# Moving the planned place of a few TensorE steps in an attention and mixture-of-experts kernel

## The chip, the cores and the metric

The kernel runs on one core of one Trainium2 chip. The metric is device time of one execution in microseconds; a run's time is a median over executions. The kernel before has a median of 804.08 us in 3 runs (800.58 to 804.29).

## The reference, cut to what matters

```python
def reference(q, k, v, w_gate, w1, w2):      # q, k, v: [8, 8, 576, 64]
    scores = q @ k.T / 8, masked in blocks of 64
    x = softmax(scores) @ v                  # as rows: [4608, 512]
    logits = x @ w_gate                      # 8 experts
    # pairs (row, expert) by falling logit; a row goes to the first expert
    # that still has room; each expert takes cap = 4608 // 8 = 576 rows
    for e in range(8):
        h = np.maximum(x[assigned == e] @ w1[e], 0.0)    # 512 -> 1024
        out[assigned == e] = h @ w2[e]                   # 1024 -> 512
```

The assignment is exact: an expert fills up, its rows leave the competition, and the next expert to fill is found.

## The kernel before, in words

**Two stages.** Attention comes first (to about 340 us in the profile) and writes its rows x in a high and a low float16 half to DRAM. Then come eight rounds k = 0 to 7, each with a routing and the products of one expert. A round's number is the order in which experts fill up, so expert 0 in this text is the first one to fill.

**Routing (`route`, `invert`).** For k < 7 a search of 14 steps finds the expert that fills next and its threshold. Each step is two counts on VectorE (L776, L777), one on ScalarE (L750) and a small matmul that adds them up (`tot`, L791), so it goes round three engines. Then VectorE makes a mask, a group of matmuls gives each chosen row its place in the list (`po`, L852 to L859), VectorE turns the places into one-hot tables (L870, L872, L893 `OH`, L897 `OL`, L899 and L900 `RH`), 36 matmuls invert them (`pe`, L908), 8 more finish the list of rows (`ps`, L915), and VectorE writes it as `ix` (L918). The last routing (k = 7) has no search, since one expert is left, but all that comes after.

**Gathering (`gather`, `flip`).** Five indirect DMAs on GpSimd (L980) fetch the 576 rows of an expert as `xg`: four of 128 rows and one of 64. For k = 0 and 1 TensorE transposes each (`xt`, 8 matmuls, L990), and ScalarE (L994) and VectorE (L995) each copy one half of the result into `X`. For k > 1 a DMA on SyncE transposes (L1005).

**Weights (`weights`).** Eight loads of 512 KB (L966, SyncE) into six buffers `raw`; for the first four loads of rounds 0 and 1 ScalarE and VectorE convert (L938, L940), else ScalarE (L945, L949) and GpSimd (L951).

**Products (`ffn`).** First `h` (L1030): 8 groups over the first 256 columns of X, which needs only the first two gathered blocks, then 8 over the other 320 (128 and 448 in round 0). ScalarE and VectorE write each group out as `HH` and `HL` (L1016, L1018). Then `y`: four blocks of 128 rows, each 8 steps of 3 matmuls (L1055), and the block m = 4 with the last 64 rows, 4 steps of 6 matmuls at half width (L1059). A result leaves through ScalarE (L1038, for m = 4 also VectorE, L1042) and an indirect DMA on GpSimd (L1046). PSUM has four buffers `g` for h and y.

**What sets the order.** Every engine carries out its instructions in the order in which the program holds them, and that order is made at build time by a planner (`Sched`). Each strand of the work is a generator that names an engine, a cost in ns and the events that it waits for; `Sched.run` takes the strand that could start first by its own clock, and lets one of higher priority (smaller number) go first where it becomes ready soon enough: for TensorE in this stage, more than 500 ns (`ST`) before the other would have ended. A strand that has been ready for over 300 ns (`WAIT`) is not held back further. Transposes have priority 1, products 3, routing 0. The planner's clock is a guess: on the chip, semaphores hold the instructions until their inputs are there, in the planned order.

A gather tells the planner by `soft` (L65) when its rows will have landed: `q`, the planner's clock of the DMA queue, is set to the later of `q` and now plus `lat` (1100 ns), plus a cost of 728 ns, and the event stands 950 ns after that. `hold` (L886) sets an event that the matmuls `po` (L848) and `pe` (L903) of a routing wait for; it is called once ahead of each of the two.

Of the kernel before, what the change touches and what calls it, by code (L numbers as in the profile page):

```python
# [614 lines left out]
class Moe:  # L615
# [269 lines left out]
        yield from s.invert(k,L16,h2)  # L885
    def hold(s,k):  # L886

        s.sc.ev['hold',k]=s.sc.now+(8000 if k==s.E-1 else 0)
    def invert(s,k,L16,h2):
        nc=s.nc; rp=s.rp; C=s.C; V=nc.vector; sc=s.sc  # L890
        yield D,440
# [80 lines left out]
    def gather(s,k,ix):  # L972
        nc=s.nc; fp=s.fp; sc=s.sc
        tl=[]
        for m in range(5):
            n=P if m<4 else 64
            yield G,1038,('ffn',k-2),('xm',k-1,m)
            if m==0: X=s.X[k]=fp.tile([P,8,576],F16,tag="X",name=f"X{k}")
            xg=fp.tile([P,1024],F16,tag="xg",name=f"xg{k}_{m}",bufs=5)
            nc.gpsimd.indirect_dma_start(out=xg[:n],out_offset=None,in_=s.xd,in_offset=bass.IndirectOffsetOnAxis(ap=ix[:n,m:m+1],axis=0))  # L980
            sc.soft(728,('xg',k,m))
            sc.nolat()
            if m==4: sc.set(('gi',k))
            sc.add(s.flip(k,m,n,xg,X),1,sc.now)
# [138 lines left out]
```

## Time and profile before

| what | value |
| --- | --- |
| median of 3 runs | 804.08 us (800.58 to 804.29) |
| the profiled execution's own time | 801.86 us |
| its span, first to last instruction | 800.1 us |
| TensorE busy, share of the span | 717.8 us, 90% |
| VectorE, ScalarE, GpSimd busy | 585.0, 545.1, 467.0 us |
| mean granted TensorE clock | 0.965 |

The span is what the trace covers; 1.76 us of the profiled execution lie outside it. The median of the runs is 2.2 us above the profiled execution, which lies inside their spread. PE stands for TensorE, DVE for VectorE, ACT for ScalarE, POOL for GpSimd, SP for SyncE; a row of a timeline has the start in us, the duration in us, engine, line, operation, output and inputs, a shape, a count, and in brackets the idle time of the engine ahead of it and what ended that. In a timeline, neighbouring instructions of the same line and tiles are merged.

### The profile page before, as it was taken

How to read it: one execution, taken by the hardware profiler on the slowest of the kernel's cores; microseconds unless marked ns; L12 is line 12 of the kernel's file. 1: busy time of each engine (PE TensorE's matmuls, PEld its weight loads, DVE VectorE, ACT ScalarE, POOL GpSimd, SP SyncE). 2: the span in 40 equal slices, each digit the busy share in tenths (PEclk: the TensorE clock that was granted, in tenths of full speed). 3: DMA queues.
4: the chain of work that ended last, by engine and by line, in shares of the span. 5: the costliest groups of instructions: out<-in, count | busy, mean ns of one | idle time of the engine just before them, and what ended most of it. 6: DMA issues, size and time to landing. Idle time of an engine off the chain costs nothing.

```text
span 800.1 us, 19136 instructions
## 1 busy us (share of the span) xinstructions
PE 717.8 (90%) x6539; PEld 479.6 (60%) x6539; DVE 585.0 (73%) x2395; ACT 545.1 (68%) x1476; POOL 467.0 (58%) x509
## 2 busy tenths in 40 slices
PE   5889998899999999913898999999999999999995
PEld 3666676677767767601644755747557475574752
DVE  6899798988889799488787977969777683730210
ACT  5789888888988888533745859496775947392210
POOL 5788888897889876212324337475471926873001
PEclk9899999999999999955899999999999999999998
DMA  9879999999999991324408049291845819861001
GB/s 203 157 145 179 213 203 209 164 176 204 230 164 222 188 198 35 99 80 133 138 14 294 25 139 231 74 295 42 254 129 184 179 49 273 270 162 40 20 15 45
DMA packets 244305, 121.51 MB, mean 152 GB/s; under 512 B 200816, under 2 KB 227312, under 8 KB 244208
## 3 DMA queue, kind: packets, MB, share of 16 engines
q1 hardware_dynamic: 238320, 101.42, 56.1%
q0 software_dynamic: 5888, 18.88, 7.4%
q8 instruction: 51, 0.84, 0.4%
q14 instruction: 46, 0.38, 0.2%
HBM read 71.32 MB, written 18.87 MB: 113 GB/s over the span
## 4 chain that ended last, share of the span: by engine, by line
PE 58%; DVE 19%; DMA 8%; ACT 8%; issue 3%; POOL 3%; SPq 1%; POOLq 0%; DVEq 0%; ACTq 0%
PE h L1030 23%; PE y L1055 16%; PE psb L463 5%; DVE m L405 5%; PE psb L380 4%; DMA kT<-k 4%; PE psb L498 4%; ACT P L416 4%; DVE kS L350 2%; POOL P L438 2%; PE y L1059 2%; DMA xg<-x,ix 2%; ACT PT L444 2%; DVE jk L776 1%; DMA raw<-in_moe_w_dram 1%
## 5 line engine op out<-in xcount | busy, mean ns | idle before, releaser
L438 POOL TENSOR_TENSOR P<-P,m 128x320 f32<-128x320 f32 (+8 forms) x285 | 209.3, 769 | 48.2 <-DVE m L430 28.4
L1030 PE MATMUL h<-X,W 128*128 128x320 f16 (+3 forms) x1536 | 195.1, 287 | 0.0
L1030 PEld LDWEIGHTS <-W 128*128 128x128 f16 x1536 | 142.2, 98 | 42.7 <-issue 3.1
L416 ACT ACTIVATE P<-psb,m 128x576 f32<-128x576 f32 (+8 forms) x288 | 149.2, 542 | 25.8 <-DVE m L409 19.7
L1055 PE MATMUL y<-W,HH 128*128 128x512 f16 x512 | 152.2, 379 | 0.0
L951 POOL TENSOR_TENSOR W<-raw,W 128x1024 f16<-128x1024 f32 x56 | 118.4, 2136 | 40.6 <-ACT W L949 38.3
L405 DVE TENSOR_REDUCE m<-psb 128x1 f32<-128x576 f32 (+8 forms) x288 | 125.0, 481 | 12.4 <-PE psb L380 11.9
L463 PE MATMUL psb<-mident,P 128*128 128x128 f32 x800 | 106.0, 281 | 10.9 <-POOL P L438 3.6
L1046 POOL DMA_INDIRECT out_dram<-yo,ix x40 | 39.4, 986 | 113.1 <-ACT yo L1038 79.2
L380 PEld LDWEIGHTS <-qT 128*64 128x64 f16 x1408 | 78.1, 112 | 42.8 <-issue 27.8
L380 PE MATMUL psb<-kT,qT 128*64 128x288 f16 (+8 forms) x704 | 91.7, 286 | 10.2 <-ACT P L416 9.7
L463 PEld LDWEIGHTS psb<-mident,P 128*128 128x128 f32 x800 | 87.3, 142 | 22.5 <-POOL P L438 6.4
L498 PE MATMUL psb<-PT,V 128*64 128x448 f32 (+5 forms) x776 | 97.2, 388 | 2.4 <-DVE PT L446 1.9
L980 POOL DMA_INDIRECT xg<-x,ix x40 | 41.6, 1040 | 95.8 <-DVE ix L918 37.7
L1055 PE MATMUL y<-W,HL 128*128 128x512 f16 x256 | 97.0, 379 | 0.0
L1016 ACT ACTIVATE HH<-h 128x320 f16<-128x320 f32 (+3 forms) x128 | 52.1, 410 | 63.9 <-PE h L1030 59.5
L444 ACT ACTIVATE PT<-psb 128x512 f32<-128x512 f32 (+1 forms) x165 | 82.4, 592 | 5.8 <-PE psb L463 5.6
L380 PE MATMUL psb<-kS,qT 128*64 128x288 f16 (+8 forms) x704 | 84.4, 284 | 1.6 <-DVE kS L350 1.5
L1018 DVE SCALAR_TENSOR_TENSOR HL<-h,HH 128x320 f16<-128x320 f32 (+3 forms) x128 | 56.9, 452 | 38.5 <-ACT HH L1016 38.2
L1055 PEld LDWEIGHTS <-HH 128*128 128x128 f16 x512 | 46.9, 98 | 52.6 <-issue 2.0
L945 ACT ACTIVATE raw<-raw 128x512 f32<-128x512 f32 x112 | 67.4, 626 | 6.6 <-DMA raw<-in_moe_w_dram 6.5
L498 PEld LDWEIGHTS psb<-PT,V 128*64 128x64 f32 x776 | 49.5, 137 | 33.5 <-issue 24.3
(204 smaller groups left out, 1074.9 us busy)
## 6 DMA issues: line engine op xcount, KB each, us to landing
raw<-in_moe_w_dram SPq DMA_DIRECT2D x64, 512.0 KB, 5.5
x<-XR SPq DMA_DIRECT2D x8, 1152.0 KB, 5.7
kn<-in_k_dram SPq DMA_DIRECT2D x15, 576.0 KB, 5.1
qn<-in_q_dram SPq DMA_DIRECT2D x15, 576.0 KB, 7.1
V<-in_v_dram SPq DMA_DIRECT2D x64, 128.0 KB, 4.4
V<-in_v_dram SPq DMA_DIRECT2D x16, 64.0 KB, 3.9
xg<-x,ix POOLq DMA_INDIRECT x40, 4.3
out_dram<-yo,ix POOLq DMA_INDIRECT x40, 2.8
```

The costliest lines, as they stand in the source:

```text
L380: nc.tensor.matmul(out if len(K1.shape) == 2 else out.rearrange("p (r j) -> p r j", r=2), lhsT=A[:, h, 64 * i:64 * i + 64], rhs=K1, start= ...
L405: nc.vector.tensor_reduce(m[:, 0, c:c + 1], ps[:, o:o + 64 * (i + 1)] if g else s.part(ps, g, i, o), axis=AX.X if g else AX.XY, op=OP.max)
L416: nc.scalar.activation(out, in_, AF.Exp, bias=m[:, 1, c:c + 1], scale=s.ESC, accum_out=m[:, 2, c:c + 1])
L438: nc.gpsimd.tensor_tensor(sl, sl, m[:, 3, c:c + 1].to_broadcast([P, w]), op=OP.mult)
L444: s.nc.scalar.activation(out, in_, AF.Copy)
L463: nc.tensor.transpose(ps[:, a], s.Pb[n % s.NP][:, s.OFF[i] + 128 * j:s.OFF[i] + 128 * j + P], s.ident)
L498: nc.tensor.matmul(ps[64 * h:64 * h + 64, 64 * (i0 - b0):64 * (b1 - b0)], lhsT=vn[:, j, 2 * (n % 2) + h, :], rhs=pt[:, s.PTI[(j, i0)]:s.PT ...
L945: nc.scalar.activation(raw[:,x],raw[:,x],AF.Copy,scale=s.WS)
L951: nc.gpsimd.tensor_tensor(lw,raw,hi,op=OP.subtract)
L1018: nc.vector.scalar_tensor_tensor(HL[:,f,ts],ps,0.0,HH[:,f,ts],op0=OP.max,op1=OP.subtract)
L1030: nc.tensor.matmul(ps,lhsT=W[:,a,d,f*P:f*P+P],rhs=X[:,4*(d//2)+d%2+l,ts],start=(d==0 and n==0),stop=(d==3 and n==2))
L1055: if m<4: nc.tensor.matmul(ps,lhsT=Z[:,f,m*P:m*P+P],rhs=Y[:,a,f],start=(f==n==0),stop=(f==7 and n==2))
```

## The change

Two numbers that only the planner reads are changed. No instruction is added, removed or altered; only the order of the instructions on the engines can differ.

```diff
     def hold(s,k):
 
-        s.sc.ev['hold',k]=s.sc.now+(8000 if k==s.E-1 else 0)
+        s.sc.ev['hold',k]=s.sc.now+(10000 if k==s.E-1 else 0)
...
             nc.gpsimd.indirect_dma_start(out=xg[:n],out_offset=None,in_=s.xd,in_offset=bass.IndirectOffsetOnAxis(ap=ix[:n,m:m+1],axis=0))
-            sc.soft(728,('xg',k,m))
+
+            sc.soft(728,('xg',k,m),4600 if k==1 else 1100)
             sc.nolat()
```

The first edit is about the last routing (k = 7): each of `po` and `pe` is held for 10.0 us of the planner's clock instead of 8.0. The second is about the second expert (k = 1): its gathers count as landed at the earliest 4600 + 728 + 950 ns after their issue instead of 1100 + 728 + 950 ns. By its description the change puts the products of the first expert's last 64 rows ahead of the transposes of the second expert's rows, and the last routing's matmuls later.

## The prediction

> **What bounds the kernel now.** I read the page first, then busy time by stage, then TensorE's waits, and last the timelines of the two places that the change touches.
>
> ```profile
> PE 717.8 (90%) x6539; PEld 479.6 (60%) x6539; DVE 585.0 (73%) x2395; ACT 545.1 (68%) x1476; POOL 467.0 (58%) x509
> core 0: us, PE busy (x) PEld busy (x) DVE busy (x) ACT busy (x) POOL busy (x), PEclk, DMA share, GB/s
> 432.90:443.63 10.73, 6.92 (x72) 3.65 (x71) 7.85 (x37) 5.20 (x13) 4.17 (x4) 1.00 0.64 231
> 443.63:493.33 49.70, 49.70 (x384) 30.64 (x382) 41.12 (x225) 38.99 (x96) 24.38 (x16) 1.00 0.46 140
> engine line waited for: us in total, times, longest us
> PE xt L990 <- DMA xg<-x,ix: 3.5, 3, 1.7
> PE pe L908 <- DVE RH L900: 1.3, 1, 1.3
> PE tot L791 <- ACT ja L750: 1.3, 2, 0.7
> ```
>
> In the expert stage TensorE is the bound: from 443.63 to 493.33 it is busy for all 49.70 us. So time is won only where it stands still, and a microsecond won there reaches the end unless something else becomes late. The waits (window 432.9 to 700) name the places. Two belong to the change: 3.5 us in front of `xt`, the transposes of the second expert's rows, all in the stretch 432.90 to 443.63 (6.92 busy of 10.73), and 1.3 us in front of `pe` of the last routing. The third, 1.3 us, is the search, in the rounds between. Nothing else is above 0.2. So the stretch from 443.63 to the last routing is almost solid, and what the change can win lies in 3.5 + 1.3 us and what hangs on them. The clock is 1.00 in both stretches shown, so a shorter wait changes no clock.
>
> **Edit for k = 1: products ahead of transposes.** TensorE's order at that place:
>
> ```profile
> 434.86 0.62 PE L990 MATMUL xt<-m_idh,xg 128*128 128x128 f16 x8 [1.75 <-DMA xg<-x,ix]
> 436.29 0.62 PE L990 MATMUL xt<-m_idh,xg 128*128 128x128 f16 x8 [0.81 <-DMA xg<-x,ix]
> 436.75 0.59 PE L1055 MATMUL y<-W,HH 128*128 128x512 f16 x2
> 438.53 0.62 PE L990 MATMUL xt<-m_idh,xg 128*128 128x128 f16 x8 [0.97 <-DMA xg<-x,ix]
> 440.12 1.03 PE L990 MATMUL xt<-m_idh,xg 128*128 128x128 f16 x16
> 441.09 0.62 PE L1059 MATMUL y<-W,HH 128*64 128x512 f16 x4
> 441.76 0.60 PE L1059 MATMUL y<-W,HH 128*64 128x512 f16 x4
> 443.63 1.81 PE L1030 MATMUL h<-X,W 128*128 128x256 f16 x15
> 432.95 0.95 POOL L980 DMA_INDIRECT xg<-x,ix  x1 [0.30 <-issue]
> 434.20 1.23 POOL L980 DMA_INDIRECT xg<-x,ix  x1 [0.30 <-issue]
> DMA to landing us min/median/max: 7.1/7.1/7.1
> DMA to landing us min/median/max: 6.5/6.5/6.5
> ```
>
> (The last four rows are the gathers of the fourth and fifth block, and what the view of line 980 gives for each alone.) In the old order the last product step of block m = 3 and the four steps of the last 64 rows (L1059) stand between and behind the transposes, while TensorE stands at transposes whose rows haven't landed. The planner had expected them 1100 + 728 + 950 = 2778 ns after the issue; with the change it expects them at 6278 ns at the earliest, close to the 6.5 and 7.1 us above. The shift is at most 3.5 us. The five product steps need 5 x 0.67 = 3.3 us (the step at 441.76 follows the one at 441.09 by 0.67; the step of m = 3 is taken alike). So all of them just fit ahead.
>
> What then bounds the start of `h` at 443.63? The transposes still can't run before their rows land, and the landing doesn't move: the gathers are issued on POOL by 435.4, before anything differs. From 434.86 - 1.75 = 433.11, where the old order fell idle, TensorE has 3.3 us of products and two transposes at 1.03 / 2 = 0.52, together 4.4 us: done by 437.5, the first landings (434.86, 436.29) long past, with 1.0 us to spare for two small `tot`. The third transpose waits for its landing at 438.53, the fourth for 432.95 + 7.1 = 440.05, the fifth for 434.20 + 6.5 = 440.7. It ends at 440.7 + 0.5 = 441.2, and `h` follows: 443.63 - 441.2 = **2.4 us earlier**. The bounds: if the planner keeps one product step of 0.67 behind the last transpose, 1.7; if it also lets steps of `h`, whose first half needs two blocks only, into the waits for the fourth and fifth, all the idle time of the stretch, 10.73 - 6.92 = 3.8, can go. I take 2.4, the row of the last landing, since the shift of 3.5 barely exceeds the 3.3 us of work: little is left to slip in front.
>
> `h` needs two more things. Its weights:
>
> ```profile
> 440.23 1.22 DVE L940 SCALAR_TENSOR_TENSOR W<-raw,W 128x1024 f16<-128x1024 f32 x1
> 463.41 2.13 POOL L951 TENSOR_TENSOR W<-raw,W 128x1024 f16<-128x1024 f32 x1 [1.16 <-ACT W L949]
> 471.89 0.59 PE L1055 MATMUL y<-W,HH 128*128 128x512 f16 x2
> ```
>
> The last conversion of W1 ends at 441.45 on DVE, queued behind the copies out of `xt`; with the copies planned later it can only move forward, and where it stays it costs 0.2. The last conversion of W2 ends on POOL at 465.54, and its first user, the seventh step of `y`, stands at 471.89: 6.35 us of cover. PE comes 2.4 us earlier, and the planner, which has the loads behind the transposes, may order the conversions up to 3.5 us later: 0.4 are left, so I cost it at nothing. The copies (L994, L995) stand later on ACT and DVE; the search step behind them, whose `tot` stands behind the first transpose in PE's queue until now, comes earlier, so nobody waits for the move. The `g` buffers that m = 4 and `h` take over were emptied before, except block m = 3's, which now ends earlier. The queues passed are PE, ACT and DVE; SP and POOL hold nothing that the move passes.
>
> **Edit for the last routing.** VectorE and GpSimd there, with the same two instructions one round earlier in the first two rows:
>
> ```profile
> 659.56 0.18 DVE L870 TENSOR_SCALAR h<-q 128x36 f16<-128x36 f32 x1
> 661.55 0.75 DVE L897 TENSOR_TENSOR OL<-m_iom,L 128x1152 f16<-128x1152 f16 x1
> 680.04 0.18 PE L853 MATMUL po<-MM,m_tri 128*128 128x36 f16 x1
> 680.55 5.25 DVE L870 TENSOR_SCALAR h<-q 128x36 f16<-128x36 f32 x1
> 686.41 5.38 DVE L897 TENSOR_TENSOR OL<-m_iom,L 128x1152 f16<-128x1152 f16 x1
> 692.16 0.40 DVE L900 TENSOR_SCALAR RH<-OH,m_pc 128x720 f16<-128x720 f16 x1
> 679.46 6.30 POOL L951 TENSOR_TENSOR W<-raw,W 128x1024 f16<-128x1024 f32 x3
> 686.96 4.21 POOL L951 TENSOR_TENSOR W<-raw,W 128x1024 f16<-128x1024 f32 x2
> 692.61 0.91 PE L908 MATMUL pe<-RH,OL 128*32 128x40 f16 x36 [1.35 <-DVE RH L900]
> 693.45 0.62 PE L1059 MATMUL y<-W,HH 128*64 128x512 f16 x4
> 696.44 23.69 PE L1030 MATMUL h<-X,W 128*128 128x256 f16 x192
> 710.68 6.31 SPq L1005 DMA_TRANSPOSE X<-xg  x4
> 743.50 23.69 PE L1030 MATMUL h<-X,W 128*128 128x256 f16 x192
> ```
>
> Between `po` and `RH` lie 12.5 us, of which two instructions take 10.6 instead of 0.9: each ends when a run of POOL's L951 ends (685.80 beside 679.46 + 6.30 = 685.76; 691.79 shortly behind 686.96 + 4.21 = 691.17). The planner knows nothing of this; it puts `pe` 8 us behind its own end of `RH`, and PE stands for 1.35 us. With the change `po` moves 2.0 us back (to 682.0) and `pe` 4.0, since its hold counts from steps that follow `po`: from its old place, 691.26, to about 695.2, behind the four steps of the last 64 rows and one or two of expert 6's `h`.
>
> When is `RH` ready then? L870 comes to 682.6, still within POOL's run until 685.76; so all behind it stays, and `RH` ends at 692.56: cover 2.7 us. If instead these instructions take 10.6 us of themselves, `RH` ends 2 us later, at 694.6, and 0.6 us of cover are left. Either way the wait of **1.35 us goes**; for it to stay whole, `RH` would have to come 4 us late, so the term lies between 0 and 1.35. The Trainium skill ("SBUF — State Buffer", section "Terms") has VectorE and GpSimd share a port pair that is locked for a whole instruction, while the loser blocks; by it the first reading holds, by the plain durations the second, and with 0.6 us to spare instead of 2.7 this term would be less sure. The ends at 685.80 and 685.76 agree with the rule.
>
> What `pe` passes, and what its followers pass, costs nothing: the list `ix` feeds the gathers of expert 7, whose `h` starts at 743.50; the last of its transposing DMAs is issued by 710.68 + 6.31 = 717.0, which leaves 26 us, and 4 are used. POOL's stores and conversions queued behind the gathers serve the same `h` or the output of rows long done.
>
> **Sum.** 801.86 - 2.4 - 1.35 = 798.1 for an execution like the profiled one; that one lies 2.2 us under the median of the runs, so the median becomes 804.08 - 3.75, rounded **800.4 us**, 0.47% less. About 0.5%, 4.0 us, is what a measurement of this kernel can tell from no change.
>
> **Rivals.** *More idle time goes*: `h` fills the waits between landings (3.8 instead of 2.4), and the search, no longer held up behind transposes, takes away its 1.3 later on: 804.08 - 3.8 - 1.35 - 1.3 = 797.6. For it: routing runs on with less delay. Against: the plan's shift hardly exceeds the work.
>
> *The change does only half*: the transposes stay in front, or the 2.4 us are taken back by the W2 conversions, whose cover falls to 0.4. Then 804.08 - 1.35 = 802.7. The planner's 500 ns rule, which lets a transpose past a step that it would meet, speaks for the first; the 0.4 still being cover, against the second.
>
> *A descriptor delay*: the gather at 430.69 took 1.95 us on POOL where that at 432.95 took 0.95. If rearranged DVE work does this to the last one, `h` loses 1.0: 801.4. L940 moves forward, and its like ran there (430.60 in the row below). The Trainium skill ("SBUF — State Buffer", section "SBUF: two separate sides") lets some VectorE instructions keep GpSimd from writing the descriptors of its DMAs; these two rows agree. Against: by the old trace DVE comes to its next L940 only after the last gather's issue.
>
> ```profile
> 430.60 1.22 DVE L940 SCALAR_TENSOR_TENSOR W<-raw,W 128x1024 f16<-128x1024 f32 x1
> 430.69 1.95 POOL L980 DMA_INDIRECT xg<-x,ix  x1 [0.30 <-issue]
> 587.65 0.16 PE L791 MATMUL tot<-cn,m_bo 128*128 128x3 f16 x1 [0.58 <-ACT ja L750]
> 579.14 6.20 DMA raw<-in_moe_w_dram
> ```
>
> *Slower*: the planner's moved clock gives experts 2 to 6 another order. SP issues loads and transposing DMAs in one queue; at 579.14 a load came late behind them and took 6.20 us; ACT had to wait for it, a sign count stood behind that on ACT, and PE stood for the count (0.58 at 587.65). If one more DMA that waits for a gather comes ahead of such a load, ACT stands up to 6.2 us and PE 5.6 more than now. It decides from 3.75 us on: once is 804.08 - 3.75 + 5.6 = 805.9, twice 811.5. Against it: a planned tie that has to fall badly, and `mid` ties each routing to the products two rounds before, so that shifts don't add up.
>
> **Chances.** Forecast 0.50, more goes 0.22, half or a delay 0.18, slower 0.10 (0.07 of it past 0.5%). The forecast's 0.47% lies just under the bound, so about four in ten of it count as faster; with nearly all of the second case: faster 0.42, same 0.51, slower 0.07. Range: down to 797.6 and a little for the spread of 0.2% in the runs, 796.8; up to no gain, 804.1.
>
> **What would show it.** Right: no wait of `xt` above 1.1 us and together under 2; five product steps ahead of the second transpose; `h` of expert 1 at about 441.2; no wait at `pe`, with L1059 all in front of it; L870 still ending with POOL's run; `h` of expert 6 at 692.7, the span 796.4. Wrong: `h` of expert 1 at 443 or later, new waits on `raw` or on W2 in PE's list between 443 and 690, or `RH` behind `pe` again.

## The result, and the profile after

| | before | changed |
| --- | --- | --- |
| median | 804.18 us (6 runs, 800.58 to 807.52) | 811.95 us (6 runs, 810.18 to 814.58) |
| ratio to before | | 1.0109, 95% interval 1.0083 to 1.0135 |
| span of the profiled execution | 800.1 us | 810.4 us |
| mean granted TensorE clock | 0.965 | 0.957 |

The changed kernel is 1.1% slower; 0.47% faster was forecast. Lines from L981 on stand one later in the changed kernel (`h` is L1031, the 64-row steps L1060, stores L1047). First its list of TensorE's waits, for the window 420 to 812: engine, line, what it waited for, us in total, times, longest.

```profile
PE h L1031 <- POOL W L951: 7.4, 1, 7.4
PE tot L791 <- ACT ja L750: 4.8, 6, 1.7
PE xt L991 <- DMA xg<-x,ix: 1.7, 3, 1.1
PE tot L791 <- DVE jk L777: 0.3, 1, 0.3
```

Against the list of before, the wait of `pe` (1.3) is gone and that of `xt` halved (3.5 to 1.7): both intended effects are there. New is one wait of 7.4 us of `h` for a weight conversion on GpSimd, and the search's waits, `tot`, grew from 1.5 (1.3 + 0.2) to 5.1. Next TensorE's timeline of the changed kernel, at the place of the edit for k = 1 and at the long wait.

```profile
434.33 0.62 PE L1060 MATMUL y<-W,HH 128*64 128x512 f16 x4
435.75 0.62 PE L991 MATMUL xt<-m_idh,xg 128*128 128x128 f16 x8
436.30 0.62 PE L1060 MATMUL y<-W,HH 128*64 128x512 f16 x4
...
440.85 0.62 PE L991 MATMUL xt<-m_idh,xg 128*128 128x128 f16 x8 [1.06 <-DMA xg<-x,ix]
441.33 0.81 PE L1031 MATMUL h<-X,W 128*128 128x256 f16 x6
...
493.03 0.16 PE L791 MATMUL tot<-cn,m_bo 128*128 128x3 f16 x1 [1.10 <-ACT ja L750]
493.06 1.36 PE L1031 MATMUL h<-X,W 128*128 128x256 f16 x11
501.81 1.04 PE L1031 MATMUL h<-X,W 128*128 128x256 f16 x4 [7.39 <-POOL W L951]
707.00 0.92 PE L908 MATMUL pe<-RH,OL 128*32 128x40 f16 x36
```

`h` of the second expert starts at 441.33 (before 443.63). `h` of the third starts at 493.06, still 0.27 us ahead of before, does 11 matmuls, and stands until 501.81. Why, GpSimd's timeline tells, first of the changed kernel, then of before:

```profile
484.73 6.31 POOL L951 TENSOR_TENSOR W<-raw,W 128x1024 f16<-128x1024 f32 x3
491.20 1.00 POOL L1047 DMA_INDIRECT out_dram<-yo,ix  x1 [0.17 <-issue]
498.64 0.96 POOL L1047 DMA_INDIRECT out_dram<-yo,ix  x1 [6.43 <-DMA X<-xg]
499.62 6.29 POOL L951 TENSOR_TENSOR W<-raw,W 128x1024 f16<-128x1024 f32 x3
```

```profile
484.19 2.15 POOL L951 TENSOR_TENSOR W<-raw,W 128x1024 f16<-128x1024 f32 x1
486.51 1.01 POOL L1046 DMA_INDIRECT out_dram<-yo,ix  x1 [0.17 <-ACT W L949]
487.55 6.32 POOL L951 TENSOR_TENSOR W<-raw,W 128x1024 f16<-128x1024 f32 x3
494.03 1.01 POOL L1046 DMA_INDIRECT out_dram<-yo,ix  x1 [0.17 <-issue]
499.55 0.96 POOL L1046 DMA_INDIRECT out_dram<-yo,ix  x1 [4.52 <-ACT HH L1016]
```

W1 of an expert is four conversions (L951), and the fourth is wanted by the 12th matmul of `h`. Before, all four ended by 493.87, ahead of the stores of the second expert's third and fourth block. Now three stand ahead of the two stores and the fourth behind them, at 499.62. The second store waits 6.43 us, and the conversion, ready long since, waits in GpSimd's queue behind it. The chain of waits of the changed kernel (start, duration, what) runs through the first store's landing:

```profile
491.20 6.67 DMA out_dram<-yo,ix
...
498.64 0.96 POOL out_dram L1047
...
499.62 2.14 POOL W L951
...
501.81 1.04 PE h L1031 x4
```

The clock adds to it. Windows of the changed kernel, with the columns of the prediction's second view:

```profile
494.00:496.00 2.00, 0.42 (x4) 0.12 (x2) 1.76 (x9) 2.00 (x6) 0.00 (x0) 0.80 1.04 265
496.00:498.00 2.00, 0.00 (x0) 0.00 (x0) 0.00 (x0) 0.13 (x1) 0.00 (x0) 0.50 1.00 134
501.80:506.00 4.20, 4.19 (x24) 3.10 (x25) 1.95 (x11) 2.87 (x7) 4.11 (x2) 0.57 0.02 6
```

TensorE works from 501.80 to 506.00 at 0.57, so 4.20 x 0.43 = 1.8 us of work are lost there. The DMA share of about 1.0 while the store is under way says that the 16 DMA engines were busy throughout, with the transposing DMAs among the rest; that this made the landing late (6.67 us, where the profile's page gives 2.7 as the median of all 40 stores) is argued, not shown. The Trainium skill ("DMA: Bandwidth & Descriptors", section "Anatomy of one DMA — SWDGE (gpsimd) path") says that a DMA's semaphore wait happens on the sequencer that issues it, ahead of its dispatch; the 6.43 us on POOL, with work behind them, agree.

**The balance.** Stall 7.4, lost clock 1.8, search 5.1 - 1.5 = 3.6, less 1.8 at the transposes and 1.3 at `pe`: 9.7 of the 810.4 - 800.1 = 10.3 us between the spans. The two spans are single executions, and the medians lie 7.8 us apart, so this is an account of the profiles and not of the medians.

### The profile page after: what moved, and what is told of

Read it like the earlier page. It is cut to its first block, busy times and chain, and to the rows that moved or that the text cites. A ratio compares the mean times of both kernels' runs of the same rounds, so it can differ in the third digit from the quotient of the medians.

```text
span 810.4 us, 19131 instructions
## 1 busy us (share of the span) xinstructions
PE 718.8 (89%) x6539; PEld 480.0 (59%) x6539; DVE 579.1 (71%) x2395; ACT 546.8 (67%) x1476; POOL 465.1 (57%) x509
## 4 chain that ended last, share of the span: by engine, by line
PE 52%; DVE 17%; DMA 10%; ACT 8%; POOL 6%; issue 5%; SPq 1%; POOLq 0%; DVEq 0%; ACTq 0%
PE h L1031 21%; PE y L1056 13%; DVE m L405 5%; PE psb L463 5%; DMA kT<-k 4%; PE psb L498 4%; ACT P L416 4%; PE psb L380 4%; DMA raw<-in_moe_w_dram 4%; PE y L1060 2%; DVE kS L350 2%; POOL xg L980 2%; POOL W L951 2%; POOL P L438 2%; ACT PT L444 2%
## 5 line engine op out<-in xcount | busy, mean ns | idle before, releaser
L1031 PE MATMUL h<-X,W 128*128 128x320 f16 (+3 forms) x1536 | 198.6, 290 | 7.4 <-POOL W L951 7.4
L1031 PEld LDWEIGHTS <-W 128*128 128x128 f16 x1536 | 144.0, 100 | 50.9 <-POOL W L951 7.7
L951 POOL TENSOR_TENSOR W<-raw,W 128x1024 f16<-128x1024 f32 x56 | 117.9, 2135 | 24.2 <-ACT W L949 23.9
L1047 POOL DMA_INDIRECT out_dram<-yo,ix x40 | 38.8, 971 | 120.4 <-ACT yo L1039 76.1
L380 PE MATMUL psb<-kS,qT 128*64 128x288 f16 (+8 forms) x704 | 82.7, 280 | 1.7 <-DVE kS L350 1.5
```

What stands on the lines that cost most here:

```text
L380: nc.tensor.matmul(out if len(K1.shape) == 2 else out.rearrange("p (r j) -> p r j", r=2), lhsT=A[:, h, 64 * i:64 * i + 64], rhs=K1, start= ...
L951: nc.gpsimd.tensor_tensor(lw,raw,hi,op=OP.subtract)
L1031: nc.tensor.matmul(ps,lhsT=W[:,a,d,f*P:f*P+P],rhs=X[:,4*(d//2)+d%2+l,ts],start=(d==0 and n==0),stop=(d==3 and n==2))
```

## The experiments

My theory after the result: the whole loss is the place of that one conversion on GpSimd; the edits themselves do what they were forecast to do. Rivals: one of the edits loses in its own place, or the rest of the shifted plan does. The runs were made in three groups, each with runs of the kernel before beside them (medians 807.84, 806.90 and 803.19 us), so times are compared within a group only; the ratios are those on record, which aren't exactly the quotients of the two medians.

### One edit alone

The first kernel is before with the last-routing edit alone:

```diff
-        s.sc.ev['hold',k]=s.sc.now+(8000 if k==s.E-1 else 0)
+        s.sc.ev['hold',k]=s.sc.now+(10000 if k==s.E-1 else 0)
```

> The kernel before with the edit for the last routing alone. All theories of the loss put it into the edit for k = 1, so this one should show the small term of the prediction: no wait at pe (1.35 us before), the span 1.35 us shorter, ratio 0.998. If the later pe were part of the loss, the ratio would be above 1.003.

Measured: 806.06 us beside 807.84, ratio 0.9971 (0.9950 to 0.9991). So 2.3 us are won (0.7 to 4.0), with the forecast 1.35 inside the interval, and the wait of `pe` is gone.

The second is before with the edit for k = 1 alone:

```diff
-            sc.soft(728,('xg',k,m))
+            sc.soft(728,('xg',k,m),4600 if k==1 else 1100)
```

> The kernel before with the edit for k = 1 alone. Theory (GpSimd's order): the planner now puts expert 2's last W1 conversion behind the stores of expert 1's blocks m = 2 and m = 3, the second store waits for the landing of the first, and TensorE stands for 7.4 us in expert 2's h: the stall is there in full, and the ratio is that of the whole change plus 1.35 us, 1.011 to 1.014. Rival (the two edits meet): without the later hold the stall is not there, ratio 0.997.

Measured: 816.08 us, ratio 1.0101 (1.0069 to 1.0133). The loss belongs to this edit. GpSimd shows the same pair of stores (the second at 498.57 behind a wait of 5.83) and the conversion behind them. TensorE's timeline of this kernel:

```profile
489.11 0.16 PE L791 MATMUL tot<-cn,m_bo 128*128 128x3 f16 x1 [2.18 <-ACT ja L750]
497.39 0.18 PE L791 MATMUL tot<-cn,m_bo 128*128 128x3 f16 x1 [0.93 <-DVE jk L777]
501.74 1.04 PE L1030 MATMUL h<-X,W 128*128 128x256 f16 x4 [2.94 <-POOL W L951]
```

The ratio lies just below the 1.011 to 1.014 expected. The wait for GpSimd is shorter here, 2.94 us, because `h` of the third expert was late already: it started about 4 us later than in the changed kernel, behind waits of the search and a stretch with a clock of 0.53 (490.20 to 493.80). The stall ends at about the same time.

### The conversion moved by hand, both ways

The changed kernel with the one conversion ahead of the two stores:

```diff
+                if (k,n)==(2,3):
+                    for f in s.kept: f()
+                    s.kept=None
...
+            if k==1 and m in (2,3) and s.kept is not None: s.kept.append(store)
+            else: store()
```

> The changed kernel with one GpSimd instruction moved: expert 2's last W1 conversion stands ahead of the stores of expert 1's blocks m = 2 and 3 instead of behind them; every other engine has the same order. Theory (GpSimd's order): the 7.4 us stall of TensorE and the half clock behind it (10.2 us at 0.50, some 2.5 us) go, leaving 811.95 - 7.4 - 2.5 = 802, ratio 0.995 to 1.000. Rival (what is late is the load or ScalarE's half of the conversion, since the planner's DMA clock moved): the stall stays above 4 us, ratio above 1.005.

Measured: 806.45 us beside 807.84, ratio 0.9986 (0.9965 to 1.0006); no wait of `h` on GpSimd is left.

And the kernel before with that conversion behind the two stores:

```diff
+                def sub(): nc.gpsimd.tensor_tensor(lw,raw,hi,op=OP.subtract)
+                if (k,n)==(2,3): s.kept=sub
+                else: sub()
...
+            if (k,m)==(1,3): s.kept()
```

> The kernel before with one GpSimd instruction moved the other way: expert 2's last W1 conversion behind the stores of expert 1's blocks m = 2 and 3; neither edit, every other engine as before. Theory (GpSimd's order): a stall of 6 to 8 us in expert 2's h and a stretch at half clock behind it, ratio 1.010 to 1.014. Rival (the stall needs the earlier products of the edit): the conversion hides as the one behind it does now, ratio below 1.004.

Measured: 816.29 us, ratio 1.0100 (1.0065 to 1.0134). Its row on TensorE (`h` is L1032 here):

```profile
503.64 3.59 PE L1032 MATMUL h<-X,W 128*128 128x256 f16 x16 [6.05 <-POOL W L951]
```

So one instruction's place on GpSimd is worth 1.2% taken out of the changed kernel, and 1.0% put into the old one. That part of the theory stands. But 0.9986 (0.9965 to 1.0006) is not the 0.9953 of the prediction's sum: the gain is missing even without the stall.

### What the store waits for

The profile names a transposing DMA (`X<-xg`) as what ended the second store's wait. The changed kernel with the first of the two stores left out:

```diff
-            nc.gpsimd.indirect_dma_start(out=s.out, ...)
+            if (k,m)!=(1,2): nc.gpsimd.indirect_dma_start(out=s.out, ...)
```

> This is the changed kernel with one store left out: the third block of 128 rows of the second expert isn't written to the output; every other instruction stands where it stood. In the changed kernel GpSimd waited 6.4 us there, before the next store (L1047 at 498.64), and a weight conversion behind it came late, so that h of the third expert stood for 7.4 us; the profile's rows name a transposing DMA as what ended GpSimd's wait. Theory (the second store waits for the landing of the first, 6.67 us after its issue): with the first one gone the conversion starts 6 to 7 us earlier, the wait of h on GpSimd falls from 7.4 us to under 0.5, the span to 801 to 806, and the time to 0.995 to 1.002 of the kernel before. Rival (the store waits for the transposing DMAs, whatever store stands ahead of it): the wait of h stays above 5 us and the time at 1.006 to 1.011; only the 1.0 us that the store itself takes on GpSimd is saved.

GpSimd's timeline of this kernel:

```profile
485.60 6.29 POOL L951 TENSOR_TENSOR W<-raw,W 128x1024 f16<-128x1024 f32 x3
493.00 1.00 POOL L1047 DMA_INDIRECT out_dram<-yo,ix  x1 [1.10 <-ACT yo L1039]
494.02 6.31 POOL L951 TENSOR_TENSOR W<-raw,W 128x1024 f16<-128x1024 f32 x3
```

Measured: 807.53 us beside 806.90, ratio 1.0015 (0.9996 to 1.0035). The remaining store waits 1.10 us for its own data, the conversion starts at 494.02, and `h` doesn't wait for it. So nearly all of the 6.4 us was the landing of the store ahead, which came at 497.87 in the changed kernel (491.20 + 6.67); the row's name was only what came last by the profile, and the 0.8 us from there to 498.64 aren't explained. Two stores write the same tensor `out`, and the program lets the second wait for the first.

### A planner that knows this wait

The planner asks for the landing of store number `ny - 1`, read when the strand pauses; two stores that pause together both name the one before the pair. Here it takes the latest store's landing at the time of choosing:

```diff
+            if e == 'ys':
+                e = ('yo', s.ys)
...
-            yield G,1038,('yo',s.ny-1),('gi',1) if k==0 and m>1 else None
+            yield G,1038,'ys',('gi',1) if k==0 and m>1 else None
...
-            ... s.ny+=1
+            ... sc.ys=s.ny; s.ny+=1
```

> This is the changed kernel whose planner takes the landing of the latest store as what a store waits for (before, it took the number of the latest store when the strand paused, so that for two stores that became due together it did not see the second one's wait). The plan then puts the two conversions of the third expert between the two stores. Theory (the order on GpSimd made the loss): no wait of h on GpSimd above 1 us, and the time at 0.994 to 1.000 of the kernel before, about where the changed kernel with the one conversion placed by hand came out (0.9986). Rival (the plan's new order has its cost anyway, whichever of the two stands first): the time stays above 1.004.

Its GpSimd timeline (the store is L1050 here, the conversion L954):

```profile
489.83 1.00 POOL L1050 DMA_INDIRECT out_dram<-yo,ix  x1 [0.17 <-ACT W L952]
490.86 4.22 POOL L954 TENSOR_TENSOR W<-raw,W 128x1024 f16<-128x1024 f32 x2
496.45 0.98 POOL L1050 DMA_INDIRECT out_dram<-yo,ix  x1 [1.36 <-DMA out_dram<-yo,ix]
```

Measured: 806.73 us beside 806.90, ratio 1.0003 (0.9984 to 1.0022), a little above what was expected. The two conversions now stand in the time of the landing, the stall is gone, and this row names the landing itself. Again only the loss is taken back.

### Another number

The changed kernel with 4100 and with 4800 ns in place of 4600; two (4100) or three (4800) of the 64-row steps still stand ahead of the first transpose, and the fourth conversion stands ahead of the two stores in both:

```diff
-            sc.soft(728,('xg',k,m),4600 if k==1 else 1100)
+            sc.soft(728,('xg',k,m),4100 if k==1 else 1100)
```

> This is the changed kernel with 4100 ns instead of 4600 in the edit for k = 1. In the plan two of the steps with 64 rows still stand ahead of the first transpose, as with 4600, but GpSimd's order for the third expert is that of the kernel before: the fourth conversion ahead of the two stores. Theory A (the order on GpSimd is the whole loss, and the intended gain of both edits is real): h of the second expert starts 1.5 to 2.9 us earlier, no wait of h on GpSimd above 1 us, and the time is 0.9945 to 0.9965 of the kernel before. Theory B (the order on GpSimd is the loss, but what the edit for k = 1 wins in its place is given back in later waits of the search): h of the second expert starts earlier all the same, tot waits 3 us or more in all between 443 and 700, and the time is 0.997 to 1.000, no better than the last-routing edit alone (0.9971).

> This is the changed kernel with 4800 ns instead of 4600 in the edit for k = 1. The plan puts three instead of two of the steps with 64 rows ahead of the first transpose, so the intended part is done more fully, and GpSimd's order for the third expert is again that of the kernel before. If the number itself were at fault (products too far ahead of the transposes), this one would be slower than 4600: 1.010 or more. Theory A (the order on GpSimd is the whole loss): no wait of h on GpSimd above 1 us, 0.9945 to 0.9975. Theory B (gain given back later): 0.997 to 1.000.

Measured: 803.51 us with 4100, ratio 0.9947 (0.9922 to 0.9972), and 802.04 us with 4800, ratio 0.9954 (0.9929 to 0.9979), beside 806.90. Both lie in theory A's range, and both are faster than the changed kernel and the one before. With 4800 the rows at the two places are, TensorE first:

```profile
434.93 0.60 PE L1060 MATMUL y<-W,HH 128*64 128x512 f16 x4
435.67 0.62 PE L991 MATMUL xt<-m_idh,xg 128*128 128x128 f16 x8
440.81 1.16 PE L1031 MATMUL h<-X,W 128*128 128x256 f16 x9
```

```profile
485.09 6.32 POOL L951 TENSOR_TENSOR W<-raw,W 128x1024 f16<-128x1024 f32 x3
491.57 1.00 POOL L1047 DMA_INDIRECT out_dram<-yo,ix  x1 [0.17 <-issue]
497.22 0.96 POOL L1047 DMA_INDIRECT out_dram<-yo,ix  x1 [4.65 <-ACT HH L1017]
```

The second store waits here too, 4.65 us, and nobody minds: what stands behind it are conversions of W2, wanted much later.

The kernel before with 4800 alone, the last routing as it was:

```diff
-            sc.soft(728,('xg',k,m))
+            sc.soft(728,('xg',k,m),4800 if k==1 else 1100)
```

> This is the kernel before with the edit for k = 1 alone, at 4800 ns instead of 4600; the last routing keeps its 8000. With both edits the number 4800 gave 0.9954, the last-routing edit alone 0.9971. Theory (each edit wins what its place allows, the two add up): 0.997 to 0.9985, and the wait of pe is back at 1.3 us or so. Rival (the products ahead of the transposes win nothing that lasts to the end): 0.9995 or more.

Measured: 800.99 us beside 803.19, ratio 0.9967 (0.9946 to 0.9988). So products ahead of the transposes win 2.6 us (1.0 to 4.3) by themselves, and with the 2.3 us of the other edit the two add up to what the kernels with both won, within the intervals.

### What keeps 4600 from the gain

Repaired kernels with 4600 stay at 0.9986 to 1.0015. One suspect was the store of the second expert's second block, which 4600 puts ahead of the third expert's first conversion. The changed kernel with GpSimd's order there put back to that of before:

```diff
+        ... s.kept=[]; s.defer=[(1,1)]
...
+                if (k,n) in ((2,0),(2,3)):
+                    for f in s.kept: f()
+                    s.kept=[]; s.defer=[(1,2),(1,3)] if n==0 else []
...
+            if (k,m) in s.defer: s.kept.append(store)
+            else: store()
```

> This is the changed kernel in which GpSimd's order for the third expert's first four conversions and the second expert's stores is put back by hand to that of the kernel before: the store of the second expert's second block behind the first conversion (the changed kernel has it ahead), and the stores of its third and fourth block behind the fourth. The kernel with only the last conversion put ahead came to 0.9986 and had a wait of tot of 1.97 us at 487.58, behind an output copy on ScalarE that stood for 2.05 us shortly after that early store's issue; four kernels with the early store show that wait, those with 4100 and 4800 ns, which have the store behind the conversion, show none and came to 0.9947 and 0.9954. Theory (the early store has a price of its own of about 2 us): no wait of tot above 1 us between 480 and 492, and the time at 0.9945 to 0.9965. Rival (the rest of the shifted plan takes it): 0.998 or more, as with the conversion alone.

Measured: 805.01 us beside 803.19, ratio 1.0018 (0.9996 to 1.0040). The reverse, before with that one store early:

```diff
+                def sub(): nc.gpsimd.tensor_tensor(lw,raw,hi,op=OP.subtract)
+                if (k,n)==(2,0): s.kept=sub
+                else: sub()
...
+            if (k,m)==(1,1): s.kept()
```

> This is the kernel before with one pair exchanged on GpSimd: the store of the second expert's second block stands ahead of the third expert's first conversion instead of behind it. Theory (the early store has a price of its own of about 2 us): tot waits 1.5 to 2.5 us for ScalarE about 5 us behind the store's issue, and the time is 1.002 to 1.004 of the kernel before. Rival (the pair's order is free): no such wait, and 0.9985 to 1.0015.

Measured: 803.43 us beside 803.19, ratio 1.0003 (0.9979 to 1.0028), and no wait of `tot` between 480 and 520. The early store is free: my theory for this part fell, the rival holds. What the kernels with 4600 share is in TensorE's waits (window 436 to 700); here those of `tot` in the kernel with GpSimd's order of before, then in that with 4800 alone:

```profile
PE tot L791 <- ACT ja L750: 5.7, 7, 1.3
...
PE tot L791 <- DVE jk L777: 1.1, 2, 0.8
```

```profile
...
PE tot L791 <- DVE jk L777: 0.2, 1, 0.2
```

All waits of `tot`, whatever ended them, added up in each kernel's one profile: 5.1 (changed), 6.4 (edit for k = 1 alone), 7.5, 7.2, 6.9 and 6.8 us (its four repairs); against 1.5 in before and 0.2 to 3.4 in the six other kernels. The means are 6.7 and 2.2, and the difference, 4.4 us, is 0.55% of the time: about what separates 0.995 from 1.000. That is an account of single profiles; no run takes these waits out. One such place, in the changed kernel and then in before, ScalarE's timeline:

```profile
490.71 1.19 ACT L945 ACTIVATE raw<-raw 128x512 f32<-128x512 f32 x2
491.81 0.61 ACT L949 ACTIVATE W<-raw 128x512 f16<-128x512 f32 x1
492.33 0.55 ACT L750 ACTIVATE ja<-m_PB,cd 128x324 f16<-128x324 f32 x1
```

```profile
491.55 0.58 ACT L1038 ACTIVATE yo<-y 128x512 f32<-128x512 f32 x1
492.03 1.14 ACT L949 ACTIVATE W<-raw 128x512 f16<-128x512 f32 x2
493.07 0.56 ACT L750 ACTIVATE ja<-m_PB,cd 128x324 f16<-128x324 f32 x1
```

In the changed kernel three halves of conversions stand between this sign count and the one before it, in before two halves and an output copy, so the counts come about equally far apart: 2.16 and 2.07 us. The difference is on TensorE. In the changed kernel a single 64-row step (0.84 us, from 491.09) stands between the two `tot`, ahead of `h`, hence the 1.10 us of waiting at 493.03. In before, two such steps and six matmuls of `h` stand there (2.1 us, from 491.91), and `tot` doesn't wait. So the search's steps fall otherwise between the products. Which decision of the planner turns that phase in all five rounds with 4600 and not with 4100 or 4800 wasn't tried and stays open.

## Why the prediction was wrong, point by point

- **The products ahead of the transposes.** Right in the mechanism. Four of the five steps went ahead of the second transpose and the last behind it; `h` of the second expert started at 441.33, forecast 441.2. That the two lie so close is in part luck: the prediction had `h` follow the fifth transpose, but here it started behind the fourth, whose rows landed at about 440.8 (forecast 440.05), and the fifth transpose ran six matmuls into `h`, at 442.08. In the kernel with 4800 alone `h` does follow the fifth, also at 441.33. In the changed kernel the waits of `xt` were 1.7 us in all, the longest 1.06, forecast under 2 and none above 1.1. The kernel with 4800 alone put the lasting gain at 2.6 us (1.0 to 4.3), forecast 2.4.
- **The last routing.** Right. `pe` no longer waits, all four 64-row steps stand ahead of it, and VectorE's L870 ended at 697.50, with GpSimd's run (691.16 + 6.29 = 697.45). VectorE's timeline of the changed kernel:

```profile
694.18 3.32 DVE L870 TENSOR_SCALAR h<-q 128x36 f16<-128x36 f32 x1
...
698.09 0.75 DVE L897 TENSOR_TENSOR OL<-m_iom,L 128x1152 f16<-128x1152 f16 x1
...
699.21 0.40 DVE L900 TENSOR_SCALAR RH<-OH,m_pc 128x720 f16<-128x720 f16 x1
```

  Of the prediction's two readings the first held: L870 took 3.32 us beside GpSimd's run, where the row of a round without one has 0.18. `RH` was ready at 699.61, 7.4 us ahead of `pe`. That is more cover than the forecast 2.7, since the second long instruction, L897, met no run of GpSimd here and took 0.75 us where it had taken 5.38. Alone the edit won 2.3 us (0.7 to 4.0), forecast 1.35.
- **The sum.** 3.75 us or 0.47% agrees with the kernels in which GpSimd's order stayed: 0.53% with 4100 and 0.46% with 4800, though both intervals reach from about 0.2% to 0.8%. (804.08 - 3.75 is 800.3, not 800.4.)
- **The step that failed**: "The queues passed are PE, ACT and DVE; SP and POOL hold nothing that the move passes." That was read from the instructions at the edit's place. But the edit moves the planner's clock, and the planner lays out everything after it anew. In it a store has priority 1 and a conversion 2, the stores' wait for each other is not fully counted, and in the new plan a pair of stores went ahead of the one conversion that `h` needed next: 7.4 us of stall and 1.8 of clock, some 55 us behind the edit. The search's waits, 3.6 us more than before, came with the new plan too; which of its decisions makes them stays open.
- **"So a shorter wait changes no clock"** was read from one execution. In the profiles of the last-routing edit alone and of before with the conversion behind the stores, TensorE has the old order around the transposes, and the clock was 0.53 (436.00 to 443.20) and 0.51 (437.00 to 444.00) there; in two other profiles with that order it was 1.00. So in two of four profiles the old order also ran at about half clock behind its waits for rows, and part of what the edit for k = 1 wins may be that; no run separates it. Nothing was said of a longer wait either, and the half clock after the stall cost 1.8 us.
- **The rival "slower"** had the kind of mechanism (a changed plan, an in-order queue, a DMA at its head) and gave it 0.10. It looked for it on SP, where a load stands behind transposing DMAs, and priced it at 5.6 us; it came on GpSimd, where a conversion stands behind two stores. That its price for two such waits, 811.5, lies beside 811.95 is chance. The rows for the right place were in the old trace: the second store's 4.52 us behind the first one (499.55), and four conversions that end at 493.87, while `h`, which starts at 493.33, wants the fourth after its first 11 matmuls, 1.36 us later by the changed kernel's row. The cover was 0.8 us, with a wait of 4.52 us next in the queue.
- **"*More idle time goes*"** had the search's waits vanish, and the text held that shifts don't add up. They grew to 5.1 us.

## What to carry to other kernels

When an edit changes an input of a planner and not the order itself, the place of the edit shows only the gain; the risk stands wherever the plan has a near tie, and the trace of before can price it: look on every in-order queue for an instruction with little cover that is next to one that waits long. A store that waits for the landing of the store before it should not stand directly behind it when something urgent follows: put that work between. And try the neighbouring values of such a number: here 4600 gave 1.0109, 4100 and 4800 gave 0.9947 and 0.9954.

## What the runs showed of the hardware that was not expected

A short wait can cost clock. In the changed kernel with the one conversion put ahead, TensorE stood 1.97 us for a `tot` that came at 487.58, and these are its windows behind it:

```profile
486.00:488.00 2.00, 0.42 (x3) 0.31 (x4) 1.33 (x9) 2.00 (x6) 2.00 (x2) 0.99 0.56 86
488.00:490.00 2.00, 2.00 (x6) 0.76 (x5) 1.46 (x8) 2.00 (x6) 2.00 (x2) 0.50 1.00 286
490.00:492.00 2.00, 2.00 (x9) 0.68 (x7) 0.00 (x0) 0.67 (x2) 2.00 (x2) 0.66 1.08 284
```

The clock falls to 0.50 when the matmuls are already running again. In the kernel whose planner knows the store's wait, a stand of 2.03 us at the same place left it at 1.00, and so did one of 1.89 us in the kernel with a store left out; in the kernel with the edit for k = 1 alone one of 2.18 us was followed by the 0.53 named above. The Trainium skill ("TensorE: Matmul & The Clock Gate", section "What's actually happening") has half rate come after an idle window of about 3.4 us, with a window that runs free of the kernel's start. That the same length of wait costs clock once and not another time agrees with the free-running window; that 1.97 us are enough doesn't agree with a whole window of 3.4 us without work.
